# The order of a tail: left units dealt out anew, combinations of x behind the fifth of them, last partial sums ahead of the activation combinations

## The chip, the cores and the metric

The kernel runs on one core of one Trainium2 chip. The metric is device time in microseconds. The kernel before takes 299.26 us, the median of three runs (298.78 to 299.77); the profiled execution has a span of 297.9 us. In what follows TensorE (PE) multiplies matrices and loads weights (PEld), VectorE (DVE) and ScalarE (ACT) read its results out of PSUM, GpSimd (POOL) works on SBUF alone, and SyncE (SP) issues most transfers.

## The reference

Attention with a mask from hashed signs, for 4 batches, 8 heads, 768 positions and 64 dimensions, and then a two-layer block with SiLU on the 3072 x 512 result.

```python
def _attn_ref(q, k, v, proj):
    q_bits = (np.einsum('bhsd,dk->bhsk', q, proj) > 0).astype(np.int64)
    k_bits = (np.einsum('bhsd,dk->bhsk', k, proj) > 0).astype(np.int64)
    # ... buckets from the bits
    mask = q_bucket[:, :, :, None] == k_bucket[:, :, None, :]
    scores = scale * np.matmul(q, k.transpose(0, 1, 3, 2))
    scores = np.where(mask, scores, -1000000000.0)
    # ... softmax over the last axis
    return np.matmul(attn, v)

def _moe_ref(x, w_in, w_out):          # x: 3072 x 512, w_in: 512 x 2048, w_out: 2048 x 512
    h = x @ w_in
    g = h * (1.0 / (1.0 + np.exp(-h)))
    return (g @ w_out).astype(np.float32)
```

## The kernel before

The kernel walks over all heads of all batches; the two-layer block of a batch is done beside the attention of the next. Matrix products of the block use a seven-product scheme: a 2 x 2 product of blocks is made of seven products of sums and differences ("combinations") of blocks, numbered 1 to 7, which are added to one another ("partial sums").

When the attention of the last batch (number 3) is done, two things are left: 13 units of batch 2's second product, and the whole two-layer block of batch 3. Both are done in the function `tail`. A unit is the product of 8 stationary tiles with 256 columns each (8 matmuls). Six of the 13 belong to the block of 512 rows (numbers 3, 7 and 4, two row tiles each), seven to the block of 256 rows (numbers 1, 2, 6, 5, 3, 7, 4). They come to `tail` in this order, with the indices that the change uses:

```python
        small = [lambda n=n: product(1, n, 0) for n in (1, 2, 6, 5, 3, 7, 4)]
        small[0] = then(small[0], (1, 2, al))                 # combination 2 after unit 1
        small[1] = then(small[1], (1, 4, al), (1, 3, al))     # combinations 4 and 3 after unit 2
        # ...
        late[:] = big[8:] + small      # 0..5: products 3, 3, 7, 7, 4, 4 of the block of 512 rows
                                       # 6..12: products 1, 2, 6, 5, 3, 7, 4 of the block of 256 rows
```

A unit's product goes to a PSUM bank; the last unit of a product is followed by an eviction (line L544 on VectorE, which adds an earlier partial, or L542 on ScalarE):

```python
            first = t == 0 and n in (1, 6, 7)
            if first:
                banks[ci, bank] = ps.tile([P, nt, NC], F32, tag="m" if in_head else "s" if scoring else "o",
                                          name="o2_ps", bufs=3 if in_head or scoring else 2)
            op = banks[ci, bank]
            for k in range(NK):
                nc.tensor.matmul(op[:, t, :], x[:, k, t * P : (t + 1) * P], y[:, k],      # L532
                                 start=(first and k == 0), stop=True, skip_group_check=True)
            # ...
            add = {1: None, 2: None, 6: 1, 5: 1, 3: 1, 7: 5, 4: 6}[n]
            if add is None:
                nc.scalar.mul(o, op, half_g)                                               # L542
            else:
                nc.vector.scalar_tensor_tensor(out=o, in0=op, scalar=half_g, in1=kept[ci, add],
                                               op0=ALU.mult, op1=ALU.add)                  # L544
```

The combinations of activations that follow a unit (`then`) are line L515, on VectorE in the tail. The first product of batch 3 is also a seven-product scheme. Its combinations of x, T1 to T4, each in two halves dt:

```python
        def t_comb(n, dt):
            x, y = {1: (xb(0, r1, dt), xb(0, r0, dt)), 2: (xb(1, r1, dt), T[1][:, dt]),
                    3: (xb(1, r1, dt), xb(0, r1, dt)), 4: (xb(1, r0, dt), T[2][:, dt])}[n]
            nc.vector.tensor_tensor(out=T[n][:, dt], in0=x, in1=y, op=ALU.subtract)        # L662
```

Its products (line L689, two matmuls of 384 columns for each hidden block f), copies (ScalarE), partial sums (VectorE) and Silus (ScalarE). Products 1, 6, 5 and 3 of one f accumulate one after another in one bank of three, each after the copy of the one before:

```python
        def prod(n, f):
            i = {1: 1, 6: 1, 5: 1, 3: 1, 2: 2, 7: 3, 4: 3}[n]
            first = n in (1, 2, 7)
            if first:
                bank[i, f] = ps.tile([P, NR0], F32, tag="s" if i == 1 else "m", name="h_ps", bufs=3)
            for dt in range(2):
                # ... w and x by n: 1 and 2 take xT and w_in, 4 takes T4 and w_in, 3 takes xT and a combined
                #     weight, 5, 6 and 7 take T1, T2, T3 and combined weights
                nc.tensor.matmul(bank[i, f], w, x, start=(first and dt == 0), stop=True,
                                 skip_group_check=True)                                    # L689

        def copy(n, f):        # ... ScalarE, L699: part[n, f] <- bank[1, f]
        def add(n, i, f):      # VectorE, L702: part[n, f] <- bank[i, f] + part[n, f]
        def silu(dst, x):      # ScalarE, L705
        def combs(f):          # combinations of activations: L714 and L716 on VectorE, L718 on GpSimd
        def comb4(f):          # L724 on GpSimd

        def filler(n=1):       # the next n left units
            for _ in range(n):
                if fill:
                    fill.popleft()()
                    flush()

        def old(a):
            for f in (a, a + 1):
                prod(4, f)
                add(6, 3, f)
```

The loop of the tail, in rounds of two hidden blocks (f = 0, 2, 4, 6; NK is 8), and what stands before and behind it:

```python
        for dt in range(2):
            t_comb(1, dt)
        filler(4)
        for n in (2, 3, 4):
            t_comb(n, 0)
        for f in range(0, NK, 2):
            fs = (f, f + 1)
            for g in fs:
                prod(1, g)
                copy(1, g)
            if f == 0:
                filler(3)
                for n in (2, 3, 4):
                    t_comb(n, 1)
            else:
                old(f - 2)
            for g in fs:
                prod(6, g)
                copy(6, g)
            if f:
                silu(gb(0, 1, f - 2, 2), both(6, f - 2))
                combs(f - 2)
                comb4(f - 2)
            filler()
            for g in fs:
                prod(2, g)
                add(1, 2, g)
            for g in fs:
                prod(5, g)
                copy(5, g)
            for g in fs:
                prod(7, g)
                add(5, 3, g)
                silu(gb(0, 0, g), part[1, g])
            for g in fs:
                prod(3, g)
                silu(gb(1, 0, g), bank[1, g])
            silu(gb(1, 1, f, 2), both(5, f))
            filler(1)
        filler(len(fill) - 1)
        combs(NK - 2)
        old(NK - 2)
        filler()
        silu(gb(0, 1, NK - 2, 2), both(6, NK - 2))
        comb4(NK - 2)
        # ... then the second product of batch 3, line L801, in the order of products
        for n in (1, -1, 6, -2, 2, -6, 5, -5, 7, 3, -3, -7, 4, -4):     # negative: the third row tile
            for t in range(2 if n > 0 else 1):
                last(int(n < 0), abs(n), t)
```

Of the kernel before, what the change touches and what calls it, by code (L numbers as in the profile page):

```python
# [17 lines left out]
def kernel(  # L18
# [149 lines left out]
    NK = NFT // 2  # L168
# [287 lines left out]
    def flush():  # L456
        for fn in after:
            fn()
        after.clear()
# [189 lines left out]
    def tail(fill):  # L649

        b = B - 1
        fill = deque(fill)
        T = {n: xpl.tile([P, 2, NR0], F16, tag=f"xT{n - 1}", name="tx") for n in (1, 2, 3, 4)}
        r0, r1 = slice(0, NR0), slice(NR0, S)

        def xb(i, r, dt):
            return xT[4 * b + 2 * i + dt][:, r]
# [5 lines that stand above are left out]
# [3 lines left out]
        def gb(r, c, k, n=1):  # L666
            t = G[2 * (2 * r + c) + k // 4]
            return t[:, k % 4 * NR0 : (k % 4 + n) * NR0]
# [7 lines left out]
# [6 lines that stand above are left out]
                fs = slice(f * P, (f + 1) * P)  # L682
                f2 = slice(NF + f * P, NF + (f + 1) * P)
                w, x = {1: (w_in16[:, dt, fs], xb(0, r0, dt)),
                        2: (w_in16[:, 2 + dt, fs], xb(1, r0, dt)),
                        4: (w_in16[:, 2 + dt, f2], T[4][:, dt]),
                        3: (sw[4, dt][:, fs], xb(1, r1, dt))}.get(n) or \
                    (sw[{5: 1, 6: 2, 7: 3}[n], dt][:, fs], T[{5: 1, 6: 2, 7: 3}[n]][:, dt])
                nc.tensor.matmul(bank[i, f], w, x, start=(first and dt == 0), stop=True,  # L689
                                 skip_group_check=True)  # L690

        def copy(n, f):
            if n == 1:
                part[1, f] = thp.tile([P, NR0], F32, tag="th", name="part1")
            elif f % 2 == 0:
                t = ld.tile([P, 2, NR0], F32, tag="ldq" if n == 6 else "ldk", name=f"part{n}")
                part[n, f], part[n, f + 1] = t[:, 0], t[:, 1]
                part[n, "both", f] = t
            nc.scalar.copy(out=part[n, f], in_=bank[1, f])  # L699

        def add(n, i, f):
            nc.vector.tensor_tensor(out=part[n, f], in0=bank[i, f], in1=part[n, f], op=ALU.add)  # L702

        def silu(dst, x):
            nc.scalar.activation(out=dst, in_=x, func=AF.Silu)  # L705

        def both(n, f):
            return part[n, "both", f].rearrange("p f c -> p (f c)")

        def combs(f):  # L710
            w = slice(f, f + 2)
            f16 = lambda t: t[:, w].rearrange("p f c -> p (f c)")
            s3[f // 2] = xpl.tile([P, 2 * NR0], F16, tag="xpr", name="gs3", bufs=4)
            nc.vector.tensor_tensor(out=gb(1, 0, f, 2), in0=gb(1, 0, f, 2), in1=gb(1, 1, f, 2),  # L714
                                    op=ALU.add)
            nc.vector.tensor_tensor(out=f16(s2), in0=gb(1, 0, f, 2), in1=gb(0, 0, f, 2),  # L716
                                    op=ALU.subtract)
            nc.gpsimd.tensor_tensor(out=s3[f // 2], in0=gb(1, 1, f, 2), in1=f16(s2),  # L718
                                    op=ALU.subtract)

        def comb4(f):
            w = slice(f, f + 2)
            f16 = lambda t: t[:, w].rearrange("p f c -> p (f c)")
            nc.gpsimd.tensor_tensor(out=f16(s4), in0=gb(0, 1, f, 2), in1=f16(s2),  # L724
                                    op=ALU.subtract)

        def filler(n=1):
# [7 lines that stand above are left out]
                prod(4, f)  # L735
                add(6, 3, f)

        for dt in range(2):
            t_comb(1, dt)
        filler(4)  # L740
        for n in (2, 3, 4):
            t_comb(n, 0)
        for f in range(0, NK, 2):
            fs = (f, f + 1)
            for g in fs:
                prod(1, g)
                copy(1, g)
            if f == 0:
                filler(3)
                for n in (2, 3, 4):  # L750
                    t_comb(n, 1)
            else:
                old(f - 2)
            for g in fs:
# [3 lines that stand above are left out]
                silu(gb(0, 1, f - 2, 2), both(6, f - 2))  # L758
                combs(f - 2)
                comb4(f - 2)  # L760
            filler()
            for g in fs:
                prod(2, g)
                add(1, 2, g)
# [8 lines that stand above are left out]
                prod(3, g)  # L773
                silu(gb(1, 0, g), bank[1, g])
            silu(gb(1, 1, f, 2), both(5, f))
            filler(1)
        filler(len(fill) - 1)
        combs(NK - 2)
        old(NK - 2)
        filler()  # L780
        silu(gb(0, 1, NK - 2, 2), both(6, NK - 2))
        comb4(NK - 2)

# [153 lines left out]
    for w in range(NW):  # L937
# [10 lines left out]
        n = -(-(len(moeq) - keep) // left) if len(moeq) > keep else 0  # L948
# [5 lines left out]
        if n == 1 and len(moeq) - keep < left and skip:  # L954
            n = 0
# [13 lines left out]
    act = nrm.tile([P, 1], F32, tag="act", name="act", bufs=1)  # L969
    nc.scalar.activation(out=act, in_=sc[:, 0:1], func=AF.Silu)  # L970
    tail(late)
# [1 line left out]
_INS = ['q', 'k', 'v', 'proj', 'moe_w_in', 'moe_w_out']  # L973
# [26 lines left out]
```

The softmax here doesn't subtract the row's maximum and nothing guards it: scores larger than these inputs give would overflow.

## Time and profile before

| engine | busy us of 297.9 | share |
|---|---|---|
| PE | 288.9 | 97% |
| ACT | 224.8 | 75% |
| POOL | 203.0 | 68% |
| DVE | 200.3 | 67% |
| PE weight loads | 196.4 | 66% |

The shares are averages over the whole span. The tail that the change touches begins near 243 us, where the last L480 matmul of the main part ends, and reaches to the end of the span. The lengths of matmuls in the profile are modelled and overlap the next one, so that a TensorE that is shown busy need not be at its peak; their starts say more. In a timeline a row is a group of like instructions: its start, the time it spans, engine, line, operation, output and inputs, shapes, count, and, where the engine stood idle before it, the length of that time with what ended it. In the tail between 255 and 275 us VectorE is busy 3.6 to 4.1 us and ScalarE 4.3 to 4.8 us of every 5 us.

### The profile page before, as it was taken

Reading aid. Unit: us, or ns where it says so; the run is one execution under the profiler, and the core shown is the slowest. Engines: PE = TensorE matmul, PEld = TensorE weight load, DVE = VectorE, ACT = ScalarE, POOL = GpSimd, SP = SyncE. Lnnn points to the kernel's source line nnn. Section 1 sums busy time; section 2 is a strip of 40 time slices with the busy share of each in tenths; the row PEclk is TensorE's granted clock in tenths of the full one; section 3 lists DMA queues with packets and bytes.
Section 4 is the critical chain, followed back from the end, with each engine's and each line's share of the span. In section 5 each row is a group of like instructions: output and inputs, shape, how many; then the busy total and the mean of one; then the engine's idle time right before and its main releaser. Section 6 shows DMA issues by size and latency. Waiting matters only on the chain.

```text
span 297.9 us, 7703 instructions
## 1 busy us (share of the span) xinstructions
PE 288.9 (97%) x2918; PEld 196.4 (66%) x2918; DVE 200.3 (67%) x391; ACT 224.8 (75%) x432; POOL 203.0 (68%) x240
## 2 busy tenths in 40 slices
PE   8999999999998999999999999999999998999994
PEld 2676755555666665567666888656668786666884
DVE  5787939898886454855798447955557665877332
ACT  5887998998987776877887786868888852889300
POOL 8578999279997955999357991599997930055500
PEclk9999999999999999999999999999999999999999
DMA  6999998979989238982299326103010113010023
GB/s 193 235 238 234 221 130 129 185 160 155 200 137 191 68 65 200 184 148 53 55 184 123 50 64 185 58 21 52 23 42 28 35 29 106 20 36 19 20 70 126
DMA packets 105877, 33.31 MB, mean 112 GB/s; under 512 B 90800, under 2 KB 105200, under 8 KB 105840
## 3 DMA queue, kind: packets, MB, share of 16 engines
q1 hardware_dynamic: 101456, 28.62, 48.7%
q0 software_dynamic: 4224, 4.19, 9.4%
q8 instruction: 23, 0.38, 0.6%
q14 instruction: 14, 0.11, 0.1%
q10 hardware_dynamic: 160, 0.00, 0.0%
HBM read 27.27 MB, written 6.29 MB: 113 GB/s over the span
## 4 chain that ended last, share of the span: by engine, by line
PE 91%; DVE 4%; ACT 3%; issue 1%; POOL 0%; ACTq 0%; POOLq 0%
PE h_ps L480 21%; PE s_ps L383 20%; PE o_ps L532 14%; PE o_ps L415 12%; PE h_ps L689 6%; PE o_ps L801 5%; PE o_ps L562 4%; PE bp_ps L297 3%; PE tp_ps L201 2%; ACT u L386 1%; PE warm_ps L125 1%; ACT th L490 1%; PE bp_ps L241 1%; DVE osb L544 1%; PE tp_ps L214 1%
## 5 line engine op out<-in xcount | busy, mean ns | idle before, releaser
L386 ACT ACTIVATE u<-s_ps 128x512 f16<-128x512 f32 x288 | 157.0, 610 | 29.6 <-PE s_ps L383 28.9
L415 PEld LDWEIGHTS <-u 128*128 128x128 f16 x1152 | 67.0, 98 | 37.8 <-ACT u L386 9.3
L415 PE MATMUL o_ps<-vv,u 128*128 128x65 f16 x1152 | 82.5, 194 | 0.6 <-ACT u L386 0.4
L480 PE MATMUL h_ps<-xT,win 128*128 128x512 f16 (+1 forms) x384 | 75.1, 326 | 0.0
L493 DVE SCALAR_TENSOR_TENSOR g<-th,h_ps 128x512 f16<-128x512 f32 x72 | 48.4, 680 | 37.0 <-ACT th L490 36.7
L383 PE MATMUL s_ps<-qka 128*128 128x512 f16 x192 | 52.6, 326 | 0.9 <-DVE osb L566 0.4
L383 PE MATMUL s_ps<-qkb 128*128 128x512 f16 x192 | 53.0, 326 | 0.2 <-ACT u L386 0.2
L490 ACT ACTIVATE th<-h_ps 128x512 f32<-128x512 f32 x72 | 43.8, 608 | 11.0 <-PE h_ps L480 7.6
L480 PEld LDWEIGHTS <-win 128*128 128x128 f16 x384 | 37.5, 98 | 17.9 <-issue 0.4
L532 PEld LDWEIGHTS <-g 128*128 128x128 f16 x336 | 32.8, 98 | 7.6 <-issue 1.1
L435 POOL TENSOR_TENSOR x_pr<-osum,rec 128x384 f16<-128x384 f32 x23 | 19.7, 858 | 24.7 <-DVE rec L434 23.8
L267 POOL TENSOR_SCALAR qka<-qk 64x1536 f16<-64x1536 f32 x15 | 21.9, 1463 | 17.1 <-DVE qk L262 8.4
L267 POOL TENSOR_SCALAR qkb<-qk 64x1536 f16<-64x1536 f32 x15 | 22.0, 1469 | 1.2
L532 PE MATMUL o_ps<-wout,g 128*128 128x256 f16 x168 | 21.6, 272 | 0.3 <-DVE osb L544 0.3
L532 PE MATMUL o_ps<-wt,g 128*128 128x256 f16 x168 | 21.6, 273 | 0.2
L278 POOL TENSOR_TENSOR vsa<-v_sb 128x192 f32<-128x192 f32 x32 | 18.9, 591 | 0.0
L718 POOL TENSOR_TENSOR gs<-qka,gs 128x768 f16<-128x768 f16 x2 | 3.3, 1644 | 22.4 <-ACT qka L705 22.4
L544 DVE SCALAR_TENSOR_TENSOR osb<-o_ps,osb 128x256 f32<-128x256 f32 (+1 forms) x25 | 13.1, 525 | 6.5 <-PE o_ps L532 6.4
L276 POOL CAST vv<-v_sb 128x384 f16<-128x384 f32 x32 | 16.7, 521 | 0.6
L562 PE MATMUL o_ps<-wout,g 128*128 128x512 f16 x64 | 16.4, 379 | 0.6 <-ACT u L386 0.5
L515 DVE TENSOR_TENSOR g<-g 128x1024 f16<-128x1024 f16 x15 | 14.9, 996 | 2.2 <-PE o_ps L532 2.0
L262 DVE STREAM_TRANSPOSE qk<-k_blk 128x768 f32<-128x768 f32 x10 | 15.9, 1594 | 0.0
(121 smaller groups left out, 440.7 us busy)
## 6 DMA issues: line engine op xcount, KB each, us to landing
v_sb<-in_v_dram SPq DMA_DIRECT2D x15, 384.0 KB
out_dram<-osb SPq DMA_DIRECT2D x16, 256.0 KB
q_blk<-in_q_dram SPq DMA_DIRECT2D x40, 96.0 KB
k_blk<-in_k_dram SPq DMA_DIRECT2D x40, 96.0 KB
win<-in_moe_w_in_dram POOLq DMA_DIRECT2D x4, 512.0 KB, 7.8
wout<-in_moe_w_out_dram POOLq DMA_DIRECT2D x4, 512.0 KB, 6.6
out_dram<-osb SPq DMA_DIRECT2D x16, 128.0 KB
q_sb<-in_q_dram SPq DMA_DIRECT2D x5, 384.0 KB
```

The lines of the kernel that those rows point to most:

```text
L267: nc.gpsimd.tensor_scalar(out=dst[rows, :], in0=qk32[p][rows, :], scalar1=CS, scalar2=1.0, op0=ALU.mult, op1=ALU.mult)
L278: nc.gpsimd.tensor_tensor(out=sa, in0=src[:, 0:3], in1=src[:, 3:6], op=ALU.add)
L383: nc.tensor.matmul(sp[:, o0 : o0 + n], t[:, S + jt * P : S + (jt + 1) * P], t[:, c0 : c0 + n], start=True, stop=True)
L386: nc.scalar.activation(out=u, in_=sp, func=AF.Exp, scale=ESC)
L415: nc.tensor.matmul(o_ps[h][:, c0 // P + i, :], u[:, o0 + i * P : o0 + (i + 1) * P], vv[:, jt, :], start=(not direct(h) and w % NU == 0 and ...
L435: (nc.vector if direct(h) else nc.gpsimd).tensor_tensor(out=x_pr[p][:, :, par * D : (par + 1) * D], in0=o[:, 0:NJ, 0:D], in1=rec[:, :, Non ...
L480: nc.tensor.matmul(hp[:, :, j, :], w_in16[:, dt, ft * P : (ft + 1) * P], xT[4 * b + dt][:, c0 : c0 + n] .rearrange("d (r c) -> d r c", r=2 ...
L490: nc.scalar.activation(out=th, in_=hp, func=AF.Tanh, scale=0.5)
L493: nc.vector.scalar_tensor_tensor(out=g, in0=th.rearrange("p r f c -> p r (f c)"), scalar=1.0, in1=hp.rearrange("p r f c -> p r (f c)"), op ...
L532: nc.tensor.matmul(op[:, t, :], x[:, k, t * P : (t + 1) * P], y[:, k], start=(first and k == 0), stop=True, skip_group_check=True)
L562: nc.tensor.matmul(op, x, w_out16[:, ft, :], start=(ft == 0), stop=(ft == NFT - 1))
L689: nc.tensor.matmul(bank[i, f], w, x, start=(first and dt == 0), stop=True, skip_group_check=True)
```

## The change

No instruction is added or taken away; only the order in the tail changes, in three parts. The 13 left units are dealt out anew: product 1 of the small block goes first, its product 2 before product 4 of the large block, and the units are spread over the loop so that some reach the last round. All eight combinations of x stand together behind the fifth unit instead of around the units. Behind the loop the last two partial sums (`old`) come before the last combinations of activations (`combs`). It is meant to take away waits of TensorE at the head and at the end of the tail.

```diff
@@ tail @@
-        fill = deque(fill)
+        fill = deque([fill[i] for i in (6, 0, 1, 2, 3, 7, 4, 5, 8, 9, 10, 11, 12)])
@@ ahead of the loop @@
+        filler(5)
         for dt in range(2):
-            t_comb(1, dt)
-        filler(4)
-        for n in (2, 3, 4):
-            t_comb(n, 0)
+            for n in (1, 2, 3, 4):
+                t_comb(n, dt)
+        filler()
         for f in range(0, NK, 2):
@@ in the loop, behind product 1 @@
             if f == 0:
-                filler(3)
-                for n in (2, 3, 4):
-                    t_comb(n, 1)
+                filler(2)
             else:
                 old(f - 2)
@@ in the loop, ahead of product 2 @@
-            filler()
+            if f < NK - 2:
+                filler()
@@ at the end of a round and behind the loop @@
             silu(gb(1, 1, f, 2), both(5, f))
-            filler(1)
-        filler(len(fill) - 1)
+            if f in (0, NK - 2):
+                filler()
+        old(NK - 2)
+        filler(len(fill))
         combs(NK - 2)
-        old(NK - 2)
-        filler()
         silu(gb(0, 1, NK - 2, 2), both(6, NK - 2))
         comb4(NK - 2)
```

## The prediction

> **What bounds the kernel now.** I read the page's busy shares first (TensorE 97%, ScalarE 75%, the rest near 67%), then its chain by engine (PE 91%, DVE 4%, ACT 3%). Both say that time is made of matmuls, and that a change of order can only win where TensorE stands still. All that the change touches lies after 243 us, so I read the chain of that stretch in order of time; columns are start, length, what:
>
> ```profile
> 247.11 0.70 DVE osb L544
> ...
> 247.85 2.79 PE o_ps L532 x24
> ...
> 250.67 0.69 DVE g L515
> 251.36 0.28 DVE tx L662
> ...
> 251.68 0.65 PE h_ps L689 x3
> ...
> 276.09 0.62 DVE qkb L714
> 276.73 0.56 DVE gs L716
> 277.29 0.94 DVE part L702 x2
> ```
>
> At 247 us the chain goes through an eviction, at 250.67 through a combination of old activations (L515) and then one of x (L662), at 276 through activation combinations with the last sums (L702) behind them. Next I read TensorE's timeline (start, length of the group, operands, and in brackets the idle time before with its releaser):
>
> ```profile
> 247.85 1.91 PE L532 MATMUL o_ps<-wt,g 128*128 128x256 f16 x16
> 249.59 1.04 PE L532 MATMUL o_ps<-wout,g 128*128 128x256 f16 x8
> 250.47 0.33 PE L689 MATMUL h_ps<-tx,sw 128*128 128x384 f16 x1
> 251.68 0.65 PE L689 MATMUL h_ps<-tx,sw 128*128 128x384 f16 x3 [0.89 <-DVE tx L662]
> ```
>
> The ends of matmuls are modelled and overlap, so I count by starts. From 247.85 to 249.59 sixteen of 256 columns start: 0.109 us each. Groups of four with 384 columns start 0.65 us apart (263.20, 263.85, 264.50): 0.1625 each. A start later than its predecessor plus that step is lost time. By this count TensorE loses, from the last L480 matmul on:
>
> 0.42 us before 243.42 (first left unit waits for the DVE's partial osb L544); 0.29 before 247.85 (unit 4 waits for unit 7's eviction from the same bank); 1.05 before 251.68; 0.40 before 255.06 (product 7 waits for a bank whose sum L702 stands behind the last two L515); 0.35 in four crumbs between 265 and 275.1; 0.14 before 277.81 and 0.34 before 279.90. Sum 2.99 us. From 279.90 to the last matmul there is no gap, and the eviction and output after it aren't touched.
>
> The third view is ScalarE's timeline of the tail, because every round of its loop (two hidden blocks f, f+1) puts copies and Silus there:
>
> ```profile
> 257.48 0.86 ACT L699 COPY part<-h_ps 128x384 f32<-128x384 f32 x2
> 258.73 0.86 ACT L699 COPY part<-h_ps 128x384 f32<-128x384 f32 x2 [0.38 <-PE h_ps L689]
> ...
> 260.90 0.86 ACT L699 COPY part<-h_ps 128x384 f32<-128x384 f32 x2 [0.57 <-PE h_ps L689]
> ...
> 263.95 0.88 ACT L699 COPY part<-h_ps 128x384 f32<-128x384 f32 x2
> ...
> 278.26 0.84 ACT L705 ACTIVATE qkb<-part 128x768 f16<-128x768 f32 x1 [2.20 <-DVE part L702]
> ```
>
> One round takes 263.95 - 257.48 = 6.47 us, of which 0.38 + 0.57 is waiting: 5.5 us of ScalarE. TensorE needs 28 x 0.1625 = 4.55 us for a round, plus 0.875 for each left unit of eight matmuls: 6.30 with two units, 5.42 with one, 4.55 with none. **Rounds with two units are TensorE's; with one or none they are ScalarE's.** That decides the case.
>
> **What the Trainium skill says.** "TensorE: Matmul & The Clock Gate", Back-to-back issue gap, gives N/2.4 + 2.5 ns for an isolated warm matmul: 109 ns for 256 columns, 162.5 ns for 384. The trace agrees (0.109 and 0.1625 us), though the section expects less in long pipelined streams. "PSUM — Partial Sum Buffer", Engine vs sequencer instructions, calls the ScalarE and VectorE queues strict FIFO; the trace shows it at 250.67, where the combination of x (L662), which reads no product, starts only behind the L515 that waited for TensorE. "ScalarE: Activation LUTs", What ACT_TABLE_LOAD costs, gives 186 ns + 0.833 ns an element and about 93 ns of overlap: by estimate 0.83 us for 768 columns. The trace has 0.84 to 0.87, starting 0.73 to 0.74 apart when back to back.
>
> **The change part by part.** No instruction is added or removed; left units and DVE instructions move. I call units of the 512-row block 3a, 3b, 7a, 7b, 4a, 4b, and those of the small block s1, s2, s6, s5, s3, s7, s4. Before: 3a 3b 7a 7b, then 4a 4b s1 and s2 and s6 in round 0, s5 s3 in round 2, s7 s4 in round 4, none in round 6. After: s1 3a 3b 7a 7b, then s2, then 4a 4b s6 s5 in round 0, s3 in round 2, s7 in round 4, s4 at the end of round 6.
>
> (1) Head. s1 needs no partial of the DVE, so it starts at 243.00, and 3a at 243.87, after the eviction that ended at 243.36: 0.42 saved. s2 and four products (0.875 + 0.65) stand between 7b and 4a, over the 0.69 us eviction: 0.29 saved. The eight L662 follow 7b's eviction: 7b ends near 247.5, eviction to 248.2, then 0.27 to 0.33 each, so the sixth, which product 6 needs, is done near 250.2. TensorE gets to product 6 at 247.37 + 0.875 + 0.65 + 1.75 = 250.65: 1.05 saved. Then the DVE: L662 to 250.5, two L515 to 251.7, 4b's eviction to 252.3, s6's after s6 (252.2) to 252.7, the first sum L702 to 253.25. Its bank is wanted by the second product 7 at 253.8: 0.40 saved. Round 0 ends at 255.65, TensorE without a gap: 243.00 + 10 x 0.875 + 24 x 0.1625. Head: 2.16 us won.
>
> (2) Rounds 2 to 6. In round 2 ScalarE copies product 1 until 257.2, just when TensorE wants it (round 0's long head gave it room), and with s3 round 2 ends at 261.08. Now no unit covers the turn to round 4. ScalarE still has, after product 3 ends, two Silus, one wide Silu and two copies: Silus to 261.95, wide one to 262.7, copies to 263.1 and 263.5. TensorE waits for the bank of product 1 until 261.68 (0.28), and product 6 can start at 263.15 and 263.53 rather than at 262.38 plus those 0.28 (0.50, 0.05): 0.83 lost. Round 4 with s7 is the same again: 267.33 to round 6, whose product 6 starts at 269.36 and 269.73, not 268.63: 0.78 lost. In round 6 the wait of s4 falls beside the Silus: product 3 ends at 272.66, s4 at 273.53, product 4 at 274.18. Rounds: 1.61 us lost, where before 0.35 went in crumbs.
>
> (3) End. Last sums (L702) go ahead of L714: they fill the 1.42 us in which the DVE waited for ScalarE, the Silu that began at 278.26 begins near 275.1, and the copies behind it come early. L716 ends near 276.2; the first three last products (24 x 0.1094 = 2.62 us) keep TensorE until 276.8. Both end gaps go: 0.48 saved.
>
> Sum: lost time goes from 2.99 to about 1.61, so 1.4 us won; by the times, the last product starts its final stretch at 276.80 + 144 x 0.1094 = 292.56 where it was 293.87, so 1.3. I take 1.35: 299.26 - 1.35 = **297.9 us**.
>
> **The rivals.** (a) The tail becomes gapless: all 2.99 us, 296.3 us. For it: TensorE does as much work, and each gap has its cause moved. Against: 5.5 us of ScalarE in rounds with 5.42 and 4.55 us of matmuls; I give it little. (b) The turns cost more than the head gains: after 261 us ScalarE has no slack, and a sum that comes late on the DVE (s3's and s7's evictions stand in its queue) would pass on to Silus and copies. Losing another 0.7 us at both turns gives 299.3, no change. For it: before, with a unit at the turn to round 6, product 6 came just when its copy ended (270.86 against about 270.75), so there was no reserve. (c) An output or bank wait replaces one removed: 4b's eviction needs the buffer that 3b's output left, about 5 us after its issue rather than 7. In the changed program this eviction does wait for an output; a late one would hold the DVE ahead of all the sums of round 0, 0.5 to 1 us: 298.4 to 298.9.
>
> **Range and chances.** The most to win is 2.99 us, 1%, so 2% (6 us) faster is closed by the count of gaps; 6 us slower would need four times the loss of the turns. The three runs before span 298.78 to 299.77, so half a microsecond either way is noise; (a) and (b) make 296.3 and 299.3 the outer bounds. Range 297.0 to 299.0; faster 0.01, same 0.97, slower 0.02.
>
> **What would show it.** Right: no TensorE gap over 0.15 us between 243.0 and 255.6; L662 all in one row after the two L544; two pairs of waits of TensorE for ScalarE's copies (L699), near 262 to 263.5 and near 268 to 269.7, some 0.8 us each; ScalarE without idle from 261 to 270; the last wide Silu begins before 276 us instead of at 278.26; the last matmul 1.3 us earlier. Wrong: a gap at product 6 of round 0 (the DVE's L662 late), waits at the turns well under 0.4 us (then 297 or less) or over 1.2 (then near 298.7), or an idle DVE before 4b's eviction, which is rival (c).

## The result, and the profile after

The changed kernel takes 298.32 us (median of 6 runs, 297.58 to 298.77) against 299.24 us (6 runs, 298.78 to 299.77). The ratio is 0.9968, with a 95% interval from 0.9951 to 0.9986: 0.9 us won; the interval does not reach 1, and the gain is far below 2%. Predicted were 297.9 us, range 297.0 to 299.0.

TensorE's timeline of the changed kernel (start, length of the group, operands; idle time before it in brackets), from the last matmuls of the main part to the end of round 0 and the first row of round 2:

```profile
242.13 1.04 PE L480 MATMUL h_ps<-xT,win 128*128 128x256 f16 x8
243.01 2.78 PE L532 MATMUL o_ps<-wout,g 128*128 128x256 f16 x24
245.63 1.91 PE L532 MATMUL o_ps<-wout,gd 128*128 128x256 f16 x16
...
248.90 1.91 PE L532 MATMUL o_ps<-wt,g 128*128 128x256 f16 x16
250.65 0.81 PE L689 MATMUL h_ps<-tx,sw 128*128 128x384 f16 x4
...
254.77 1.04 PE L532 MATMUL o_ps<-wt,g 128*128 128x256 f16 x8
255.64 0.81 PE L689 MATMUL h_ps<-xT,win 128*128 128x384 f16 x4
```

Counted by starts (0.1094 us for each matmul of 256 columns, 0.1625 for 384) no gap is left here: 24 x 0.1094 after 243.01 is 245.63, and round 0 ends at 255.64. The four gaps of the kernel before, 2.16 us, are gone.

The same view at the turn from round 2 to round 4, and ScalarE's timeline of that stretch:

```profile
261.12 0.49 PE L689 MATMUL h_ps<-xT,win 128*128 128x384 f16 x2
261.82 0.48 PE L689 MATMUL h_ps<-xT,win 128*128 128x384 f16 x2 [0.21 <-ACT qka L705]
262.14 0.81 PE L689 MATMUL h_ps<-tx,win 128*128 128x384 f16 x4
263.30 0.87 PE L689 MATMUL h_ps<-tx,sw 128*128 128x384 f16 x4 [0.34 <-ACT part L699]
```

```profile
261.28 0.87 ACT L705 ACTIVATE qka<-h_ps 128x384 f16<-128x384 f32 x2
262.02 0.86 ACT L705 ACTIVATE qka<-part 128x768 f16<-128x768 f32 x1
262.75 0.88 ACT L699 COPY part<-h_ps 128x384 f32<-128x384 f32 x2
```

The second product 1 waits for a bank that the first of the two Silus at 261.28 empties; product 6 waits for the first copy, which stands behind both of them and the wide Silu. By starts TensorE loses 0.38, 0.51 and 0.05 us, and the same once more at 268.18, 269.65 and 270.36. That is 1.88 us at two turns that in the kernel before, with a unit standing at each, cost next to nothing.

The chain of the changed kernel in order of time (start, length, what) shows the same turn and a new piece at the end:

```profile
262.75 0.51 ACT part L699
263.26 0.04 issue
263.30 0.87 PE h_ps L689 x4
...
287.63 4.10 DMA out_dram<-osb
...
291.85 0.43 DVE osb L812
```

In the kernel before the chain ran through VectorE at 247, 251 and 276 us; now it runs through ScalarE at the turns, and at 287.63 through an output transfer of 4.10 us, whose buffer VectorE waits for and, behind it, TensorE for 0.38 us before 292.33. All gaps together are 2.31 us, against 2.99 before. The last matmul group starts at 292.76 instead of 293.43.

### The profile page after: what moved, and what is told of

It reads as the page before. It is cut to its first block, busy times and chain, and to the rows that moved or that the text cites. A ratio compares the mean times of both kernels' runs of the same rounds, so it can differ in the third digit from the quotient of the medians.

```text
span 297.0 us, 7707 instructions
## 1 busy us (share of the span) xinstructions
PE 288.7 (97%) x2918; PEld 196.5 (66%) x2918; DVE 200.5 (68%) x391; ACT 224.6 (76%) x432; POOL 202.9 (68%) x240
## 4 chain that ended last, share of the span: by engine, by line
PE 91%; ACT 3%; DVE 2%; DMA 1%; issue 1%; POOL 0%; ACTq 0%; DVEq 0%; POOLq 0%
PE h_ps L480 21%; PE s_ps L383 20%; PE o_ps L532 14%; PE o_ps L415 12%; PE h_ps L689 5%; PE o_ps L800 4%; PE o_ps L562 4%; PE bp_ps L297 3%; PE tp_ps L201 2%; DMA out_dram<-osb 1%; ACT u L386 1%; PE warm_ps L125 1%; PE bp_ps L241 1%; ACT part L699 1%; ACT th L490 1%
## 5 line engine op out<-in xcount | busy, mean ns | idle before, releaser
L480 PE MATMUL h_ps<-xT,win 128*128 128x512 f16 (+1 forms) x384 | 75.1, 326 | 0.0
L480 PEld LDWEIGHTS <-win 128*128 128x128 f16 x384 | 37.5, 98 | 18.0 <-issue 0.4
L532 PEld LDWEIGHTS <-g 128*128 128x128 f16 x336 | 32.8, 98 | 6.8 <-issue 0.3
L532 PE MATMUL o_ps<-wt,g 128*128 128x256 f16 x168 | 21.6, 272 | 0.1
L532 PE MATMUL o_ps<-wout,g 128*128 128x256 f16 x168 | 21.4, 272 | 0.0
L383 PEld LDWEIGHTS <-qka 128*128 128x128 f16 x192 | 15.4, 97 | 0.8 <-ACT qka L254 0.6
```

The source lines that it names most:

```text
L383: nc.tensor.matmul(sp[:, o0 : o0 + n], t[:, S + jt * P : S + (jt + 1) * P], t[:, c0 : c0 + n], start=True, stop=True)
L480: nc.tensor.matmul(hp[:, :, j, :], w_in16[:, dt, ft * P : (ft + 1) * P], xT[4 * b + dt][:, c0 : c0 + n] .rearrange("d (r c) -> d r c", r=2 ...
```

## Experiments

Theory: the head and the end of the change win what was predicted, and the new dealing of the units gives most of it back, because at the turns to rounds 4 and 6 nothing covers ScalarE's queue. Rivals: the turn costs a fixed time that no unit hides; a round with one unit has no slack on ScalarE, so that the wait only moves; the output wait belongs to the change and is what was lost. Times are compared with runs of the kernel before on the same chip, by ratio; there it took 299.00 us beside runs 1 to 4 and 299.24 beside the others. There is no run 6. "Lost" is the sum of TensorE's gaps by starts, from the last L480 matmul on.

| run | median us | ratio to before (95%) | lost us in the trace |
|---|---|---|---|
| before | 299.24 | | 2.99 |
| changed | 298.32 | 0.9968 (0.9951 to 0.9986) | 2.31 |
| 1 more output buffers | 298.09 | 0.9964 (0.9953 to 0.9976) | 1.96 |
| 2 units at the turns | 296.44 | 0.9918 (0.9900 to 0.9936) | 0.64 |
| 3 copies before the wide Silu | 297.05 | 0.9941 (0.9919 to 0.9964) | 1.03 |
| 4 the end alone | 298.63 | 0.9988 (0.9979 to 0.9997) | 2.49 |
| 5 the head alone | 297.62 | 0.9939 (0.9919 to 0.9960) | 1.20 |
| 7 head and end, old dealing | 296.32 | 0.9914 (0.9899 to 0.9928) | 0.42 |
| 8 turns, other Silu behind copies | 297.70 | 0.9951 (0.9937 to 0.9965) | 1.63 |
| 9 changed kernel again | 298.15 | 0.9964 (0.9954 to 0.9973) | 2.09 |

**2, units at the turns.** The units of rounds 2 and 4 go from the middle of the round to its end:

```diff
-            if f < NK - 2:
+            if f == 0:
                 filler()
@@
-            if f in (0, NK - 2):
-                filler()
+            filler()
```

> The changed kernel, with the left units of rounds 2 and 4 moved from the middle of the round to its end. Theory (at the turn TensorE waits for ScalarE's queue of two Silus, a wide Silu and two copies, and a unit of 0.875 us put there covers it): gaps at the turns to rounds 4 and 6 fall from 0.93 us each to under 0.2, no new gap in the middle of the rounds, ScalarE's idle 0.63 us per round is used; the last matmul 1.5 to 1.8 us earlier; time about 296.7. Rival (a round with one unit has 5.42 us of matmuls against 5.5 us of ScalarE, so the wait only moves to the middle of the round): 0.5 us or less won, 297.8 or more.

TensorE's timeline at the turn from round 2 to round 4, to compare with the four rows above:

```profile
259.45 1.04 PE L532 MATMUL o_ps<-wout,g 128*128 128x256 f16 x8
260.32 0.81 PE L689 MATMUL h_ps<-xT,win 128*128 128x384 f16 x4
260.97 0.81 PE L689 MATMUL h_ps<-tx,win 128*128 128x384 f16 x4
261.62 0.81 PE L689 MATMUL h_ps<-tx,sw 128*128 128x384 f16 x4
```

The unit (L532) stands ahead of product 1 and the rows follow one another without a gap. By the ratios this is 1.5 us faster than the changed kernel. What is left are three gaps of 0.20, 0.19 and 0.13 us and crumbs. The three gaps stand in the middle of rounds 2, 4 and 6, where the rival puts them, but they are no waits for ScalarE. The first of them in TensorE's timeline and in the chain, and VectorE's timeline there:

```profile
257.30 1.67 PE L689 MATMUL h_ps<-tx,sw 128*128 128x384 f16 x8
258.80 0.81 PE L689 MATMUL h_ps<-xT,sw 128*128 128x384 f16 x4
```

```profile
258.48 1.14 PE h_ps L689 x6
```

```profile
257.40 0.56 DVE L716 TENSOR_TENSOR gs<-qka,qka 128x768 f16<-128x768 f16 x1
257.88 0.55 DVE L702 TENSOR_TENSOR part<-h_ps,part 128x384 f32<-128x384 f32 x1
```

The group of eight is products 5 and 7; by steps its seventh matmul, the first of the second product 7, is due at 258.27 and starts at 258.48. That product opens a bank of three, and the sum L702 that empties this bank ends at 258.43, held back on VectorE by L714 and L716 ahead of it. The other two gaps also end 0.05 us behind such a sum (264.10 and 269.72). It is the wait that cost the kernel before 0.40 us ahead of 255.06, in other rounds. ScalarE, with no idle time beyond 0.25 us in these rounds, is nearly full here, but TensorE waits for it only in crumbs of 0.06 us.

**3, copies before the wide Silu.** The units stay where the change put them; only ScalarE's order changes:

```diff
             for g in fs:
                 prod(1, g)
                 copy(1, g)
+            if f:
+                silu(gb(1, 1, f - 2, 2), both(5, f - 2))
@@
-            silu(gb(1, 1, f, 2), both(5, f))
+            if f == NK - 2:
+                silu(gb(1, 1, f, 2), both(5, f))
```

> The changed kernel, with the wide Silu of each round put behind the two copies of the next round's product 1 in ScalarE's order; units as in the changed kernel. Theory (ScalarE's queue): the copies come 0.73 us earlier, so the gap of 0.51 us before product 6 at each turn goes, the 0.375 us for the bank of product 1 stays; 1.0 us won, time about 297.3. Rival (the turn costs a fixed time of banks or semaphores, whatever stands in ScalarE's queue): gaps unchanged, 298.3.

TensorE's rows at the same turn, and ScalarE's below:

```profile
261.35 0.49 PE L689 MATMUL h_ps<-xT,win 128*128 128x384 f16 x2 [0.21 <-ACT qka L705]
261.67 0.81 PE L689 MATMUL h_ps<-tx,win 128*128 128x384 f16 x4
262.32 0.81 PE L689 MATMUL h_ps<-tx,sw 128*128 128x384 f16 x4
```

```profile
260.81 0.87 ACT L705 ACTIVATE qka<-h_ps 128x384 f16<-128x384 f32 x2
261.55 0.88 ACT L699 COPY part<-h_ps 128x384 f32<-128x384 f32 x2
262.30 0.87 ACT L705 ACTIVATE qka<-part 128x768 f16<-128x768 f32 x1
```

The copies now start right behind the two Silus, and product 6 follows product 4 without a gap; the wait for the bank (0.38) is as it was. A fixed cost of banks or semaphores would not have gone with an order on ScalarE, so that rival falls. With the same units in the same places, the order of one instruction on ScalarE is worth 2 x 0.51 us by the gaps that went, 0.8 us by the ratios, whose intervals overlap a little. What is left, besides the bank's 2 x 0.38, is 0.25 us before the second product 7 of round 6, behind a sum L702 as in run 2.

**7 and 5, the dealing put back.** Run 7 is the changed kernel with the units in the loop dealt as in the kernel before (one at the end of round 0, two each in rounds 2 and 4, none in round 6); run 5 is the same with the old end as well, so it is the head alone.

```diff
-            if f < NK - 2:
+            if f:
                 filler()
@@
-            if f in (0, NK - 2):
-                filler()
+            filler()
@@ run 5 only @@
-        old(NK - 2)
         filler(len(fill))
         combs(NK - 2)
+        old(NK - 2)
```

> The changed kernel with the dealing of the left units in the loop put back to that of the kernel before; head and end of the change stay. Theory: all of 2.16 us at the head and 0.48 us at the end is won, the turns cost nothing, lost time 0.3 to 0.5 us; time about 296.5, as with the units at the turns. Rival (the unit in the last round is needed to hide ScalarE at the end): a gap of 0.4 us or more before the product of s2, 297 or more.

> The kernel before with the head of the change alone: product 1 of the small block first, all eight combinations of x behind the fifth unit, product 2 ahead of product 4; in the loop the remaining units stand as in the kernel before (one at the end of round 0, two each in rounds 2 and 4, none in round 6), and the end is that of the kernel before. Theory (the head wins 2.16 us and it is the new dealing in the loop that gives part of it back at the turns): no gap at the head, no gap of 0.9 us at either turn, the crumbs and the 0.48 us at the end as in the kernel before; time about 296.9, less than the changed kernel. Rival (a tail ahead at its head runs into ScalarE whatever the dealing): gaps of 0.5 us or more in rounds 2 to 6 and 298 or more.

TensorE's timeline of run 7 at its last turn:

```profile
266.33 1.04 PE L532 MATMUL o_ps<-wt,g 128*128 128x256 f16 x8
267.20 0.81 PE L689 MATMUL h_ps<-xT,win 128*128 128x384 f16 x4
267.86 0.81 PE L689 MATMUL h_ps<-tx,win 128*128 128x384 f16 x4
268.51 0.87 PE L689 MATMUL h_ps<-tx,sw 128*128 128x384 f16 x4
```

Run 7 loses 0.42 us, all in crumbs of at most 0.14. It differs from the changed kernel in the dealing in the loop and in nothing else, and is 1.5 us faster by the ratio of the nearer of that kernel's two measurements, and 1.5 by gaps when the output's 0.38 us, which run 7 does not have, are left out: the new dealing is what costs, and the unit saved for the last round is not needed. Run 5 has only crumbs at head and turns, and the end of the kernel before, 0.14 and 0.33 us; and 0.33 more behind an output. Its median, 297.62, is 0.7 above what I expected; 0.33 us of output stand in its one trace, and the interval of its ratio (296.8 to 298.0 us) just reaches down to the 296.9.

**4, the end alone.**

```diff
-        filler(len(fill) - 1)
-        combs(NK - 2)
         old(NK - 2)
-        filler()
+        filler(len(fill))
+        combs(NK - 2)
```

> The kernel before, with only the last partial sums put ahead of the last combinations of activations. Step (3) of the prediction taken alone: the last wide Silu starts near 276.1 instead of 278.3, the gap of 0.34 us before 279.9 goes, and the 0.14 us before 277.8 stays, as it hangs on ScalarE and not on the sums; time about 298.9. Rival (the sums hold L714 back): L714 starts after 276.2 and the gap before the product of s2 grows beyond 0.14 us, time as before or slower.

From the three timelines, ScalarE's last wide Silus, VectorE's last sums and combinations, and TensorE's row of the product of s2:

```profile
274.90 1.60 ACT L705 ACTIVATE qkb<-part 128x768 f16<-128x768 f32 x2
```

```profile
274.53 1.02 DVE L702 TENSOR_TENSOR part<-h_ps,part 128x384 f32<-128x384 f32 x2 [0.16 <-PE h_ps L689]
275.80 0.60 DVE L714 TENSOR_TENSOR qkb<-qkb,qkb 128x768 f16<-128x768 f16 x1 [0.25 <-ACT qkb L705]
276.44 0.56 DVE L716 TENSOR_TENSOR gs<-qkb,qkb 128x768 f16<-128x768 f16 x1
```

```profile
277.37 1.91 PE L800 MATMUL o_ps<-wt,gs 128*128 128x256 f16 x16
```

The Silu follows the one before it at once, and both end gaps are gone (lost 2.49, 0.50 less), also the 0.14 us that I had put down to ScalarE. L714 and L716 stand as late as before against the rest (this execution reached its tail 0.30 us earlier: 275.80 + 0.30 is 276.10). So it was not L716 that the product of s2 had waited for. The first of the two sums behind it fits: in the kernel before it ended near 277.76, and the product, which opens the bank that this sum empties, began at 277.81. On this the prediction (both gaps go) was right and my expectation here wrong.

**1 and 9, the output wait.** Run 1 gives the outputs of the third row tiles of the last product two buffers of their own, in a tile that is dead by then; run 9 is the changed kernel again.

```diff
-            pool = nrm if keep else ops
-            o = pool.tile([P, nt, NC], F32, tag=f"part{ci}{n}" if keep else "osb", name="osb",
-                          bufs=1 if keep else 3)
+            pool = nrm if keep or ci else ops
+            o = pool.tile([P, nt, NC], F32,
+                          tag=f"part{ci}{n}" if keep else "osum" if ci else "osb", name="osb",
+                          bufs=1 if keep else 2 if ci else 3)
```

> The changed kernel, with two more output buffers in the last product (those of the third row tiles are taken from a dead tile). Theory (the new wait of the DVE for an output at 290 us holds TensorE 0.38 us): that wait of 1.8 us is gone, TensorE has no gap after 274.5 us, the last matmul group starts 0.4 us earlier than in the changed kernel; time about 298.0. The turns of the loop are as they were, 0.93 us lost at each. Rival (that wait was chance of one execution and costs nothing on the median): the same 298.3.

> The changed kernel once more, for a second trace. If the output wait of 1.8 us at the end belongs to the change, it stands there again with TensorE's gap of 0.38 us; if it is chance of one execution, the DVE waits less and TensorE has no gap after 274.5 us, and only the two turns of 0.93 us are left. Time 298.3.

The chain of waits (who waited for whom: total us, times, longest), of the changed kernel and then of run 9:

```profile
DVE osb L812 <- DMA out_dram<-osb: 1.8, 1, 1.8
```

```profile
DVE osb L812 <- DMA out_dram<-osb: 1.6, 1, 1.6
```

The wait stands in both; TensorE's gap behind it is 0.38 us in the first and 0.14 in the second, between the two outcomes that I had named. In run 1 neither is there. Runs 2, 3 and 4 wait 1.4, 1.4 and 1.3 us with no gap, run 5 waits 1.8 with 0.33. TensorE's gap is in each of the three traces that have one 1.46 us shorter than VectorE's wait (1.84, 1.60 and 1.79 us): so much of its idle time is free here, and what is beyond is paid by TensorE. Run 5 has the old end and the old dealing, so the wait is not a matter of the new dealing. The kernel before and run 7 did not show it in their one trace each, where the same evictions use the same three buffers. On the medians more buffers can't be told from none (0.9964 against 0.9968 and 0.9964). What makes the transfer take now less, now 4.10 us, stays open.

**8, the other wide Silu behind the copies of product 5.** On top of runs 1 and 2, an attempt on the three gaps of up to 0.20 us that run 2 had left, which I had put down to product 3 waiting for ScalarE.

```diff
             if f:
-                silu(gb(0, 1, f - 2, 2), both(6, f - 2))
                 combs(f - 2)
-                comb4(f - 2)
@@
             for g in fs:
                 prod(5, g)
                 copy(5, g)
+            if f:
+                silu(gb(0, 1, f - 2, 2), both(6, f - 2))
+                comb4(f - 2)
```

> The changed kernel with units at the turns (as in the second experiment), two more output buffers, and the other wide Silu of a round put behind the copies of product 5, which there held product 3 back 0.13 to 0.20 us in each round. Theory: these three gaps go as well, lost time under 0.2 us, time about 296.0. Rival (ScalarE has no idle time left in the rounds, so the wait only comes back at the next turn): 296.4, gaps of the same sum elsewhere.

ScalarE's copies of product 5 in round 2 and TensorE's product 6 at the next turn:

```profile
258.30 0.86 ACT L699 COPY part<-h_ps 128x384 f32<-128x384 f32 x2 [0.50 <-PE h_ps L689]
```

```profile
262.64 0.87 PE L689 MATMUL h_ps<-tx,sw 128*128 128x384 f16 x4 [0.35 <-ACT part L699]
```

The wait came back at the next turn, as the rival said, and larger: lost time is 1.63 us, not 0.64. The attempt was aimed at the wrong engine: the gap of round 2 is still there (0.22 us, second product 7, behind the sum L702 on VectorE), as the wide Silu had no part in it. In rounds 4 and 6 it is gone; TensorE gets there later, behind the wait at the turn. Whether the sums of product 2 ahead of L714 and L716 would close these gaps was not tried. The wide Silu had filled the time in which ScalarE waited for product 5. Moved behind the copies, it leaves ScalarE idle for 0.50 us and comes back at the turn, where TensorE waits 0.51 us for product 6 in spite of the unit.

## Why the prediction was right, and where it was off

**Step (1), the head: right to a few hundredths.** Units and products start where the working put them: 3a after s1, product 6 at 250.65, the end of round 0 at 255.64 (255.65 predicted). The sixth L662 ended at 250.12 (249.76 + 0.36; predicted near 250.2), half a microsecond ahead of TensorE.

**Step (2), the turns: the place and kind of the wait right, the size 0.27 us short, and the balance behind it not what decided.** Predicted were 0.83 and 0.78 us, measured 0.94 at each. The term that was mis-sized is ScalarE's part at the turn. I let each copy be done about 0.4 us after the instruction ahead of it (262.7, 263.1, 263.5), which is near the distance between two starts, 0.37 us, and took this for the time after which a result can be used. The chain shows 0.51 us for the first copy at 262.75, and TensorE starts 0.04 us after its end; the pairs start close because they overlap. "ScalarE: Activation LUTs", What ACT_TABLE_LOAD costs, would have said so: 186 + 0.833 x 384 ns is by estimate 0.506 us, as measured; the overlap is 0.14 us here, where the section has about 0.093. So each wait ended 0.14 to 0.15 us later than worked out: 261.82 for 261.68, 263.30 for 263.15. A crumb of 0.05 us in round 2 was left out. The wait being ScalarE's queue, and not a fixed cost of the turn, is shown by runs 2, 3 and 7.

What I said decides the case, 5.5 us of ScalarE against 5.42 us of matmuls in a round with one unit, did not make this loss. The sign that belonged to it, ScalarE without idle time from 261 to 270 us, failed; its timeline in the changed kernel's round 4 has

```profile
263.82 0.86 ACT L699 COPY part<-h_ps 128x384 f32<-128x384 f32 x2 [0.19 <-PE h_ps L689]
266.05 0.86 ACT L699 COPY part<-h_ps 128x384 f32<-128x384 f32 x2 [0.63 <-PE h_ps L689]
```

so that the two engines wait for each other in turn, and the round takes 6.36 us (261.12 to 267.48). Run 2 has just as many units in every round and takes 5.62 us for this one (260.32 to 265.94). The loss hung on where the unit stands in the round, not on how many there are.

**Step (3), the end: right.** The last wide Silu began at 275.42 (275.1 predicted), and both gaps went:

```profile
275.42 0.84 ACT L705 ACTIVATE qkb<-part 128x768 f16<-128x768 f32 x1 [0.57 <-DVE part L702]
```

The prediction worked the first gap out from the end of L716; as run 4 shows, it hung on the sums. Run 4 shows the same for the end alone, 0.50 us by gaps and a ratio of 0.9988 (0.9979 to 0.9997).

**The sum.** By gaps 1.38 us were predicted (2.99 less 1.61) and 0.68 came in the trace (2.99 less 2.31): 0.27 went in the turns, 0.05 in the crumb and 0.38 behind the output, which belongs to no step. Rival (c) of the prediction expected an output wait at the eviction of unit 4b at the head; none stood there, but one did at the end, which I had called untouched. Run 9, with 0.14 us behind the output, lost 2.09 us, so 0.9 won; the two ratios say 1.0 and 1.1. The last matmul came 0.67 us earlier in the first trace, not 1.3 as predicted. So by gaps half of the predicted gain came; 298.3 lies in the range because each of the missing terms is small, and the output's share of 0.14 to 0.38 us was in no step. Rivals (a) and (b) bracket the result as meant. The head was worth 2.16 us and the turns took back most of it; run 7 shows that this was a matter of the dealing and not of the kernel. The gapless tail of rival (a) did not come in the changed kernel, but with the old dealing it was near: 0.42 us lost. My argument against it, more ScalarE than TensorE in rounds with one unit, is not borne out by run 2 either, which has one unit in each of rounds 2, 4 and 6 and whose gaps are VectorE's. That the first three last products cover what ScalarE is behind after a last round without a unit fits run 7, which shows no gap there, but no run tests it alone.

## What to carry to other kernels

When filler work is moved to where an engine stands idle, ask what it covered where it was: here a unit of 0.875 us, with the products behind it, covered a queue of 2 us on ScalarE (261.28 to 263.26), and the same number of units in each round lost 2.31 us with those of rounds 2 and 4 in the middle of the round (0.38 of it behind an output) and 0.64 with them at the turns (run 2). Count lost time of TensorE by starts of matmuls, before and after, and hold the sum against the difference of times; here they agree within 0.3 us for every run, by its ratio. When an engine in strict order feeds another, the place of one long instruction in its queue can be worth as much as the filler (run 3), and moving it out of a stretch where it filled a wait costs as much (run 8). Before an instruction is moved to close a gap, find in the trace what ended that gap: in run 8 it was another engine.

## What was not expected

The first copy of a pair holds its reader for 0.51 us though the next starts 0.37 us after it. The output transfer near the end takes up to 4.10 us, VectorE stands idle for its buffer from 290.01 on, and of this idle time only what goes beyond 1.46 us reaches TensorE. And the 0.14 us before the product of s2, which looked like a wait for the combinations that it reads, went when the sums behind them were moved ahead.
